# Second MoE: its second-layer products moved behind other first-layer products, their PSUM sums alternated per step, and the rounding copies of its sums queued later

## The chip, the core and the metric

The program runs on one core of a Trainium2 chip. The metric is the device time of one execution in microseconds (us); times of several executions are given as a median. TensorE (PE in the rows, its weight loads PEld), VectorE (DVE), ScalarE (ACT) and GpSimd (POOL) each work through a queue of their own in order; SyncE (SP) issues the DMAs used here.

## What is computed

The reference chains three blocks over 2304 tokens of width 512, all in float32:

```python
x = _attn_ref(q, k, v)                       # linear attention, reshaped to 2304 x 512
for e in range(4):                           # first MoE: 4 experts, 512 -> 1024 -> 512
    h = np.maximum(x @ w1[e], 0.0)
    out += p[:, e:e + 1] * (h @ w2[e])
h = x @ w_in                                 # second MoE: 512 -> 2048 -> 512
g = np.where(h > 0.0, h, np.exp(np.minimum(h, 0.0)) - 1.0)
return g @ w_out
```

Each float32 matrix product is made of three products of rounded parts: a high part times a high part, high times low and low times high. A rounded high part is an ACT copy, the low part a subtraction of it from the value, mostly on POOL.

## The kernel before

Attention and the first expert come first (to about 704 us of the trace). Then follow 30 steps, `for i, (s, b) in enumerate(STEPS)`: s counts ten quarters of 512 hidden units (s = 0 to 5 the other three experts, s = 6 to 9 the second MoE), b three blocks of 768 tokens. Steps 18 to 29 are the second MoE; the row that starts at 802.8 us is step 18, and step 29 starts at 1194.9 us.

**First layer of a step.** It is a seven-product scheme (Strassen-Winograd) over two halves `fp` of the hidden units: 14 products, called p0 to p13 here (`product`, 6 matmuls each, L1146). Four PSUM banks A to D hold a half; B collects four of the products, and VectorE and ScalarE copy or add banks between them: p0 is copied to `s5` (ACT L1424), p1's bank B to bank A (ACT L1427, "the first layer's copy"), D becomes B + s5 after the third product (DVE L1431), C becomes B + s5 after the fifth (DVE L1442). The halves swap the banks, so p7/p8 and the next step's p0/p1 write banks of the half before.

**Activation.** `elu` (L1184 to L1186, three ACT instructions) works on the four quarters A11, A22, A21, A12 of a half when their bank is done; its `rest` (DVE L1193, L1194) is queued with the next product by `run_pend`. In steps 21 to 29 (`fast(i)`, s = 7 to 9) the second layer is a seven-product scheme too, so `rest` also forms the sums S1, S2, S3 with A21 (DVE L1198 to L1200) and S4 with A12 (L1203). `parts` (ACT L1168, POOL L1169) makes the rounded high and low part of each quarter and sum; `flush` queues what waits.

**Second layer.** The second-layer products of step i-1 stand between the first-layer products of step i. For steps 22 to 29 they are `turned_product(i-1, k)`, k = 0 to 6, 12 matmuls each (L1272), one behind each of the products in `PLACES`; they collect in two PSUM pairs X and Y, and DVE L1281 adds a finished one to `accs`. In steps 19 to 21 they are eight `group`s (L1245 to L1247, 12 matmuls, evacuated by ACT L1248), and in step 18 six `chunk`s of the first MoE. The last step's seven products stand alone at the end.

**Side work.** `tick` runs the entries of a table of 24 hooks a step; `MIXED` and `PLAIN` say up to which hook each product runs. On it stand the second MoE's weights: `w1_steps` (loads of the next quarter's first-layer weights, sums on DVE L773/L774 and POOL L778/L779, parts on ACT L757 and DVE or POOL L768), `w2_fast` (second-layer weights: sums DVE L807, parts ACT L798 and POOL L799) and, up to step 19, `turn_steps` (PE L950, ACT L951 and L968, DVE L979).

## Time and profile before

| | us |
|---|---|
| median of 3 executions (1254.35 to 1256.67) | 1254.52 |
| the profiled execution's own time | 1253.47 |
| its span, first to last instruction | 1251.6 |
| mean granted TensorE clock | 0.981 |
| steps 22 to 29 in the trace | 953.4 to 1226.0 |
| last seven second-layer products and the end | 1226.0 to 1251.6 |

A row of the timeline gives start, duration, engine, line, operation and tiles; square brackets hold the idle time of the engine before it and what ended that. A matmul's duration there is modelled and overlaps the next one's; the distance between two starts is what a matmul costs in a stream. The tables of waits count only the idle time itself, not a lower clock behind it.

### The profile page before, as it was taken

The numbers are of one execution on the slowest core, as the hardware profiler recorded it, in microseconds if no ns is written. First come the engines' busy times: TensorE is split into PE (matmuls) and PEld (weight loads), VectorE is DVE, ScalarE is ACT, GpSimd is POOL, SyncE is SP. The second block draws the span as 40 slices with busy tenths as digits, with TensorE's granted clock in tenths as the row PEclk, the third lists the DMA queues.
The fourth block names the chain that finished last, engine by engine and source line by source line (L and its number), as shares of the span: only waits on it lengthen the run. The fifth ranks groups of instructions, "written<-read, shape, count | busy, mean of one in ns | idle before, by whom it ended". The sixth has DMA issues, their size and how long they took to land.

```text
span 1251.6 us, 21084 instructions
## 1 busy us (share of the span) xinstructions
PE 1184.6 (95%) x7516; PEld 1126.3 (90%) x7516; DVE 906.8 (72%) x1516; ACT 676.1 (54%) x1430; POOL 651.1 (52%) x611
## 2 busy tenths in 40 slices
PE   7799999999999999999999999978999988989897
PEld 6788889889999999999999998868999977988897
DVE  6877887565877887877877865655557788787774
ACT  6544543244455554454554534546777656665662
POOL 4522552046476476575584632536247557556652
PEclk9999999999999999999999999989999989999898
DMA  9345557837777767676766679978655554644152
GB/s 268 109 143 171 187 196 245 307 116 258 251 254 253 248 243 261 224 247 241 245 247 244 218 279 325 322 233 262 239 182 193 206 194 168 231 157 173 53 225 89
DMA packets 157400, 272.35 MB, mean 218 GB/s; under 512 B 12784, under 2 KB 83952, under 8 KB 157296
## 3 DMA queue, kind: packets, MB, share of 16 engines
q1 hardware_dynamic: 155568, 267.87, 62.5%
q10 hardware_dynamic: 1728, 3.15, 0.7%
q8 instruction: 59, 0.97, 0.3%
q14 instruction: 45, 0.37, 0.1%
HBM read 224.83 MB, written 46.14 MB: 216 GB/s over the span
## 4 chain that ended last, share of the span: by engine, by line
PE 73%; DVE 12%; ACT 7%; issue 3%; DMA 3%; POOL 2%; SPq 0%; DVEq 0%; ACTq 0%; POOLq 0%
PE o L1361 18%; PE h L1146 13%; PE m L1146 13%; PE o L1272 7%; PE h L1005 7%; PE o L1005 6%; ACT half L1185 1%; DVE gt L1199 1%; DVE accs L1281 1%; DVE extra L1193 1%; PE o L1245 1%; PE o L1247 1%; PE o L1246 1%; DVE half L1200 1%; DVE half L1194 1%
## 5 line engine op out<-in xcount | busy, mean ns | idle before, releaser
L1146 PE MATMUL m<-xh,w1s 128*128 128x384 f32 x840 | 250.0, 341 | 12.1 <-DVE half L1194 7.8
L1146 PE MATMUL h<-xh,w1s 128*128 128x384 f32 x840 | 244.6, 337 | 9.9 <-DVE half L1194 6.2
L1146 PEld LDWEIGHTS m<-xh,w1s 128*128 128x128 f32 x840 | 156.3, 190 | 20.6 <-DVE half L1194 10.6
L1146 PEld LDWEIGHTS h<-xh,w1s 128*128 128x128 f32 x840 | 155.4, 189 | 12.5 <-DVE half L1194 6.5
L1146 PE MATMUL m<-xl,w1s 128*128 128x384 f32 x420 | 141.8, 338 | 0.0
L1146 PE MATMUL h<-xl,w1s 128*128 128x384 f32 x420 | 141.1, 336 | 0.0
L1005 PE MATMUL o<-w2t,hpa 128*128 128x512 f32 x432 | 118.4, 401 | 0.8 <-DVE hpa L1037 0.5
L1005 PE MATMUL h<-xh,w1t 128*128 128x256 f32 (+1 forms) x512 | 112.0, 297 | 0.1
L1005 PEld LDWEIGHTS h<-xh,w1t 128*128 128x128 f32 x512 | 86.1, 192 | 5.2 <-POOL w1t L442 0.3
L1361 PE MATMUL o<-w2g,xh 128*128 128x256 f32 x540 | 90.4, 282 | 0.0
L799 POOL TENSOR_TENSOR w2g<-r,w2g 128x512 fp32r<-128x512 f32 x56 | 75.8, 1362 | 26.1 <-ACT w2g L798 26.1
L1005 PEld LDWEIGHTS o<-w2t,hpa 128*128 128x128 f32 x432 | 75.6, 189 | 14.9 <-DVE hpa L1037 2.4
L1361 PE MATMUL o<-w2g,hpa 128*128 128x256 f32 x540 | 89.0, 282 | 0.0
L1361 PE MATMUL o<-w2g,xl 128*128 128x256 f32 x540 | 87.3, 282 | 0.0
L1383 DVE SCALAR_TENSOR_TENSOR accs<-o,pn,accs 128x256 f32<-128x256 f32 x180 | 75.7, 474 | 14.8 <-PE o L1361 14.2
L1146 PEld LDWEIGHTS m<-xl,w1s 128*128 128x128 f32 x420 | 79.8, 190 | 0.4
L1146 PEld LDWEIGHTS h<-xl,w1s 128*128 128x128 f32 x420 | 79.5, 189 | 0.5
L1361 PEld LDWEIGHTS o<-w2g,xh 128*128 128x128 f32 x540 | 78.0, 190 | 0.1
L1005 PE MATMUL h<-xl,w1t 128*128 128x256 f32 (+1 forms) x256 | 77.3, 302 | 0.0
L1361 PEld LDWEIGHTS o<-w2g,hpa 128*128 128x128 f32 x540 | 76.1, 190 | 0.1
L1361 PEld LDWEIGHTS o<-w2g,xl 128*128 128x128 f32 x540 | 75.6, 190 | 0.2
L1272 PE MATMUL o<-hpa,w2g 128*128 128x384 f32 x216 | 53.5, 366 | 19.9 <-DVE accs L1281 19.9
(301 smaller groups left out, 3033.7 us busy)
## 6 DMA issues: line engine op xcount, KB each, us to landing
xh<-xs SPq DMA_DIRECT2D x210, 384.0 KB, 5.3
xl<-xs SPq DMA_DIRECT2D x210, 384.0 KB, 6.0
r<-in_w_dram SPq DMA_DIRECT2D x56, 256.0 KB, 4.7
xs<-stage SPq DMA_DIRECT2D x43, 256.0 KB, 3.1
xs<-xh SPq DMA_DIRECT2D x21, 384.0 KB, 4.1
xs<-xl SPq DMA_DIRECT2D x21, 384.0 KB, 4.1
r<-scratch SPq DMA_DIRECT2D x24, 256.0 KB, 4.1
x<-in_w_in_dram SPq DMA_DIRECT2D x10, 512.0 KB, 3.8
```

Source lines behind the costliest of these rows:

```text
L799: nc.gpsimd.tensor_tensor(out=t[:, 1], in0=src, in1=t[:, 0].bitcast(F32), op=ALU.subtract)
L1005: nc.tensor.matmul(out, lhsT, rhs, **kw)
L1146: nc.tensor.matmul(dst, t[:, wl, c + dl, :], x[xl_][:, dl, :], start=(n == 0 and p < 2), stop=(n == 5), skip_group_check=True,)
L1185: nc.scalar.activation(out=t, in_=m, func=AF.Tanh, scale=-0.5)
L1193: nc.vector.scalar_tensor_tensor(out=m, in0=m, scalar=1.0, in1=t, op0=ALU.add, op1=ALU.mult)
L1194: nc.vector.scalar_tensor_tensor(out=g, in0=h, scalar=0.0, in1=m, op0=ALU.max, op1=ALU.add)
L1199: tt(out=s2, in0=s1, in1=g11, op=ALU.subtract)
L1200: tt(out=g21, in0=g21, in1=g11, op=ALU.subtract)
L1245: nc.tensor.matmul(o, w[:, 0, :], gh, start=(f == 0), stop=False)
L1272: nc.tensor.matmul(y[:, m], l, r, start=(n == 0 and k in STARTS), stop=(n == 5), skip_group_check=True)
L1361: nc.tensor.matmul(o, l, r, start=(first_write and m == 0 and c != 1), stop=(m == 5), skip_group_check=True)
L1383: nc.vector.scalar_tensor_tensor(out=a, in0=sums[x][:, c * HALF_M : (c + 1) * HALF_M], scalar=pr, in1=a, op0=ALU.mult, op1=ALU.add)
```

## The change

The diff, cut to its core (`s4` is a tile of its own for S4, which before took S1's place; the stanza for steps 18 to 21 differs only in places and hooks):

```diff
-        ("A11", "B11", "Y", (0, 0)), ("S1", "T1", "X", (1, 1)), ("S2", "T2", "Y", (0, 1)), ("S4", "B22", "X", (0, 1)),
-        ("S3", "T3", "Y", (1, 1)), ("A12", "B21", "X", (0, 0)), ("A22", "T4", "Y", (1, 0)),
+        ("A11", "B11", (0, 0)), ("S1", "T1", (1, 1)), ("S2", "T2", (0, 1)), ("S4", "B22", (0, 1)),
+        ("S3", "T3", (1, 1)), ("A12", "B21", (0, 0)), ("A22", "T4", (1, 0)),
...
-    GROUP_PLACES = (2, 3, 4, 6, 8, 9, 11, 12)
+    GROUP_PLACES, TURNED_PLACES = (1, 2, 4, 6, 8, 9, 11, 13), (1, 2, 4, 6, 8, 11, 13)
...
         def sums2():
             f1, f2 = r[0][:, 0], r[0][:, 1]
-            nc.gpsimd.tensor_tensor(out=f2[:, 2:], in0=f2[:, 2:], in1=f1[:, :2], op=ALU.subtract)
-            nc.gpsimd.tensor_tensor(out=f1[:, 2:], in0=f1[:, 2:], in1=f2[:, 2:], op=ALU.subtract)
-
+            tt = (nc.vector if s > S_MOE else nc.gpsimd).tensor_tensor
+            tt(out=f2[:, 2:], in0=f2[:, 2:], in1=f1[:, :2], op=ALU.subtract)
+            tt(out=f1[:, 2:], in0=f1[:, 2:], in1=f2[:, 2:], op=ALU.subtract)
+
+        if s > S_MOE:
+            return {
+                -5: begin, -3: lambda: lo(0), -2: sums1, -1: lambda: hi(1), 1: lambda: lo(1), 2: sums2,
+                5: lambda: hi(2), 7: lambda: lo(2), 8: lambda: hi(3), 10: lambda: lo(3),
+            }
...
-            (8, w2_parts, "B11"), (14, w2_sum, "T1"), (16, w2_parts, "T1"), (18, w2_parts, "B22"), (19, w2_sum, "T3"),
-            (21, w2_parts, "B21"), (25, w2_sum, "T2"), (27, w2_parts, "T2"), (30, w2_parts, "T3"), (31, w2_sum, "T4"),
-            (34, w2_parts, "T4"),
+            (8, w2_parts, "B11"), (13, w2_sum, "T1"), (17, w2_parts, "T1"), (18, w2_parts, "B22"), (19, w2_sum, "T3"),
+            (21, w2_parts, "B21"), (24, w2_sum, "T2"), (28, w2_parts, "T2"), (30, w2_sum, "T4"), (31, w2_parts, "T3"),
+            (35, w2_parts, "T4"),
...
-                a1, b1 = (34, 39)
+                a1, b1 = (35, 40)
...
-        op, wname, x, (th, mh) = TURNED[k]
-        t, y = w2g[s, wname], sums[x][:, :, :TB]
+        op, wname, (th, mh) = TURNED[k]
+        t, y = w2g[s, wname], sums["XY"[(i + k) % 2]][:, :, :TB]
...
+    EARLY = {1: 4, 2: 8, 5: 12, 8: 16, 9: 20, 12: 24}
...
+    TURNED_HOOKS = {**MIXED, 0: 1, 10: 18, 11: 21, 12: 22}
...
-            fill = {n: (chunk, i - 1, c) for c, n in zip(CHUNKS, (1, 3, 5, 8, 10, 12))}
-        hooks = MIXED if fast(i - 1) or turned(i - 1) else PLAIN
+            fill = {n: (chunk, i - 1, c) for c, n in zip(CHUNKS, (1, 3, 5, 8, 10, 12) if moe else (1, 2, 5, 8, 9, 12))}
+        hooks = TURNED_HOOKS if turned(i - 1) else MIXED if fast(i - 1) else PLAIN if moe else EARLY
...
                         elu(i, B_, fp, "A12")
-                        flush()
+                        if not seven:
+                            flush()
```

Up to step 17 every engine's order is the same. From step 22 on, the second-layer products stand behind p1, p2, p4, p6, p8, p11, p13 (before p1, p2, p4, p6, p8, p10, p12), and since seven products alternate between two PSUM pairs and a step starts on the other one, the first product of a step no longer takes the pair of the last product of the step before. The parts of S1, S2, S3 are queued with those of S4 and A12, behind the copy of the first layer's next half.

On VectorE, from step 23's p12 or p13 into step 24's p1, stood before (`extra`, `half` and `gt` hold the activation's terms and quarters, `r` and `w1s` the next quarter's weights, m, h and o are PSUM banks):

```order
L768 TENSOR_TENSOR w1s<-r,w1s 128x512
L1193 SCALAR_TENSOR_TENSOR half<-half 128x384
L1194 SCALAR_TENSOR_TENSOR gt<-h,half 128x384
L768 TENSOR_TENSOR w1s<-r,w1s 128x512
L773 TENSOR_TENSOR r<-r 128x256
L774 TENSOR_TENSOR r<-r 128x256
L1193 SCALAR_TENSOR_TENSOR extra<-extra,half 128x384
L1194 SCALAR_TENSOR_TENSOR half<-m,extra 128x384
L1198 TENSOR_TENSOR gt<-half,gt 128x384
L1199 TENSOR_TENSOR gt<-gt 128x384
L1200 TENSOR_TENSOR half<-half,gt 128x384
L1281 TENSOR_TENSOR accs<-o,accs 128x768
```

and stands now (the first two `rest` rows are A22's, the next pair A21's, the last pair A12's; L1290 is the addition that was L1281, L1201 and L1202 were L1193 and L1194, L1212 was L1203):

```order
L768 TENSOR_TENSOR w1s<-r,w1s 128x512
L1201 SCALAR_TENSOR_TENSOR extra<-extra,half 128x384
L1202 SCALAR_TENSOR_TENSOR half<-m,extra 128x384
L1206 TENSOR_TENSOR gt<-half,gt 128x384
L1207 TENSOR_TENSOR gt<-gt 128x384
L1208 TENSOR_TENSOR half<-half,gt 128x384
L773 TENSOR_TENSOR r<-r 128x256
L774 TENSOR_TENSOR r<-r 128x256
L1201 SCALAR_TENSOR_TENSOR half<-half 128x384
L1202 SCALAR_TENSOR_TENSOR half<-h,half 128x384
L1212 TENSOR_TENSOR s_9736<-half,gt 128x384
L1290 TENSOR_TENSOR accs<-o,accs 128x768
```

The weight sums L773 and L774 moved behind A21's rows, and the addition of the step's last second-layer product moved behind A12's three rows; the rows of A22 and one L768 stand ahead of this piece.

On ScalarE, in the middle of step 24 (from the last `elu` instruction of A12 to the parts of the half), stood before (`hpa`, `xh`, `xl` hold the rounded parts):

```order
L1186 ACTIVATE half<-half 128x384
L1168 ACTIVATE hpa<-gt 128x384
L1168 ACTIVATE xh<-gt 128x384
L1168 ACTIVATE hpa<-half 128x384
L1424 ACTIVATE extra<-h 128x384
L1427 ACTIVATE m<-h 128x384
L1168 ACTIVATE xl<-gt 128x384
L1168 ACTIVATE xl<-half 128x384
```

and stands now (L1434 and L1437 were L1424 and L1427, L1174 was L1168):

```order
L1192 ACTIVATE half<-half 128x384
L1434 ACTIVATE extra<-h 128x384
L1437 ACTIVATE m<-h 128x384
L1174 ACTIVATE hpa<-gt 128x384
L1174 ACTIVATE xh<-gt 128x384
L1174 ACTIVATE hpa<-half 128x384
L1174 ACTIVATE xl<-s_9736 128x384
L1174 ACTIVATE xl<-half 128x384
```

The three copies of S1, S2 and S3 moved behind the first layer's copy; five copies of parts now follow it in a row.

## Rows read from the trace of the kernel before

**Rows 1.** The page's busy times: us, share of the span, instructions
```profile
PE 1184.6 (95%) x7516; PEld 1126.3 (90%) x7516; DVE 906.8 (72%) x1516; ACT 676.1 (54%) x1430; POOL 651.1 (52%) x611
```
**Rows 2.** Waits of TensorE from 860 us on: total us, times, longest us
```profile
PE o L1272 <- DVE accs L1281: 22.1, 10, 3.9
PE m L1146 <- DVE half L1194: 6.8, 8, 1.4
PE h L1146 <- ACT m L1427: 3.7, 3, 1.8
PE m L1146 <- ACT h L1427: 2.0, 2, 1.4
```
**Rows 3.** Stretches: length; busy PE, PEld, DVE, ACT, POOL; clock, DMA, GB/s
```profile
953.40:983.10 29.70, 29.55 (x170) 29.07 (x169) 24.74 (x35) 21.21 (x45) 21.28 (x18) 1.00 0.52 179
983.10:1015.80 32.70, 30.05 (x171) 29.09 (x170) 27.16 (x41) 21.48 (x46) 17.38 (x16) 1.00 0.56 200
1015.80:1053.00 37.20, 32.01 (x169) 30.96 (x168) 29.21 (x42) 22.98 (x49) 24.11 (x21) 0.91 0.49 174
1053.00:1089.20 36.20, 31.84 (x170) 31.19 (x170) 26.46 (x38) 23.04 (x49) 22.32 (x19) 0.91 0.46 158
...
1194.90:1226.00 31.10, 29.56 (x169) 28.82 (x167) 22.26 (x35) 20.00 (x43) 15.83 (x14) 1.00 0.49 189
1226.00:1251.60 25.60, 17.39 (x86) 16.85 (x84) 11.92 (x17) 4.55 (x10) 6.88 (x6) 0.87 0.20 77
```
**Rows 4.** TensorE's timeline: a product, a second-layer product, and four of its waits
```profile
978.97 0.33 PE L1146 MATMUL m<-xh,w1s 128*128 128x384 f32 x1
...
980.01 0.68 PE L1272 MATMUL o<-xh,w2g 128*128 128x384 f32 x3
...
982.09 0.33 PE L1146 MATMUL h<-xh,w1s 128*128 128x384 f32 x1
...
1018.15 0.44 PE L1146 MATMUL m<-xh,w1s 128*128 128x384 f32 x1 [1.19 <-DVE half L1194]
...
1022.52 1.33 PE L1272 MATMUL o<-hpa,w2g 128*128 128x384 f32 x3 [3.06 <-DVE accs L1281]
...
1230.11 1.33 PE L1272 MATMUL o<-hpa,w2g 128*128 128x384 f32 x3 [3.89 <-DVE accs L1281]
```
**Rows 5.** VectorE's timeline over the boundary of steps 23 and 24
```profile
1011.86 0.56 DVE L1442 TENSOR_TENSOR h<-h,extra 128x384 f32<-128x384 f32 x1
...
1017.53 0.56 DVE L1194 SCALAR_TENSOR_TENSOR half<-m,extra 128x384 f32<-128x384 f32 x1
...
1020.25 1.35 DVE L1200 TENSOR_TENSOR half<-half,gt 128x384 f32<-128x384 f32 x1
1021.52 0.95 DVE L1281 TENSOR_TENSOR accs<-o,accs 128x768 f32<-128x768 f32 x1
```
**Rows 6.** ScalarE's timeline in step 21, parts of sums ahead of the first layer's copy
```profile
938.84 0.53 ACT L1168 ACTIVATE xl<-gt 128x384 fp32r<-128x384 f32 x1 [1.04 <-DVE gt L1199]
```
**Rows 7.** Lines in steps 26 to 28 (1093.2 to 1198.9 us): ns min/median/max, first and last start
```profile
L1185 ACT ACTIVATE half<-extra x12: 525/526/528, 1100.3 to 1193.9; 128x384 f32<-128x384 f32 x12
...
L1194 DVE SCALAR_TENSOR_TENSOR half<-m,extra x3: 557/558/558, 1123.6 to 1195.7; 128x384 f32<-128x384 f32 x3
...
L1199 DVE TENSOR_TENSOR gt<-gt x6: 557/1040/1540, 1107.5 to 1197.0; 128x384 f32<-128x384 f32 x6
...
L773 DVE TENSOR_TENSOR r<-r x2: 426/834/1243, 1108.5 to 1122.2; 128x256 f32<-128x256 f32 x2
...
L1169 POOL TENSOR_TENSOR xl<-gt,xl x9: 1004/1314/1385, 1093.1 to 1198.8; 128x384 fp32r<-128x384 f32 x9
...
L799 POOL TENSOR_TENSOR w2g<-r,w2g x7: 1286/1297/1618, 1141.5 to 1186.5; 128x512 fp32r<-128x512 f32 x7
```
**Rows 8.** The same three steps as one stretch, columns as in rows 3
```profile
1093.20:1198.90 105.70, 93.45 (x504) 90.80 (x504) 82.86 (x120) 67.45 (x143) 63.88 (x56) 0.95 0.44 155
```
**Rows 9.** VectorE in step 18, the longest wait that the second MoE starts with
```profile
824.62 1.77 DVE L979 TENSOR_TENSOR stage<-accs,stage 128x512 fp32r<-128x512 f32 x1 [2.20 <-ACT stage L968]
```

More of the change, by code (lines that the diff above doesn't have):

```diff
@@ L1186, in elu @@
         nc.scalar.activation(out=m, in_=m, func=AF.Exp, scale=-1.0)
+        if fast(i) and "s4" not in halves:
+            halves["s4"] = tmp.tile([P, TB], F32, tag="ek", name="s4")
         g11, g22, s1, s2 = (gt[:, k] for k in range(4))
@@ L1202, in rest @@
             elif name == "A12":
-                tt(out=s1, in0=g12, in1=s2, op=ALU.subtract)
-                todo = [(("S4", fp), s1), (("A12", fp), g12)]
+                s4 = halves["s4"]
+                tt(out=s4, in0=g12, in1=s2, op=ALU.subtract)
+                todo = [(("S4", fp), s4), (("A12", fp), g12)]
             else:
@@ L1401, in tile_attention_moe_moe @@
     for i, (s, b) in enumerate(STEPS):
-        fill = {}
+        moe, fill = s < S_MOE, {}
         if fast(i - 1):
-            one = turned_product if turned(i - 1) else second_product
-            fill = {n: (one, i - 1, k) for k, n in enumerate(PLACES)}
+            one, places = (turned_product, TURNED_PLACES) if turned(i - 1) else (second_product, PLACES)
+            fill = {n: (one, i - 1, k) for k, n in enumerate(places)}
         elif turned(i - 1):
@@ L1416, in tile_attention_moe_moe @@
             f1, f2 = 2 * fp, 2 * fp + 1
-            moe = s < S_MOE
             for p in range(len(PRODUCTS)):
```

## The prediction

> **What bounds the kernel now.** I read the page's busy times first: TensorE stands at 95% [rows 1], so only its gaps can be won. Since the engines' orders differ from step 18 on, the waits of TensorE in that stretch come next [rows 2]: ten waits of second-layer products for VectorE's addition L1281 (22.1 us), eight of first-layer products for A21's activation L1194 (6.8), five for the first layer's copy L1427 (5.7). The table of stretches then gives each step [rows 3]. An undisturbed step is worked out from starts in the timeline: a first-layer product takes 1.04 us (978.97 to 980.01), a second-layer product 2.08 (980.01 to 982.09) [rows 4], so 14 and 7 of them make 29.1. Step 22 took 29.7, step 23 32.7, step 24 37.2, step 25 36.2, step 29 31.1 [rows 3]; steps 26 to 28 repeat 23 to 25. Steps 23 to 29 (983.1 to 1226.0, 242.9 us) are 39.1 over seven undisturbed ones. At 1226 the first-layer products end and the next start comes at 1230.11 [rows 4].
>
> A wait costs more than its idle time: steps 24 and 25 and the end show granted clocks of 0.91, 0.91 and 0.87 against 1.00 [rows 3], a stay at the lower of the two levels (1.2 against 2.4 GHz) behind idle times of 3 to 4 us. Behind the wait at 1230.11 three matmuls take 1.33 us where they take 0.68 at 980.01 [rows 4]; about twelve at twice the time cost some 2 us. The end therefore loses 3.9 + 2 = about 6 us, and steps 23 to 29 and the end together 45.
>
> **The change part by part.**
>
> *The alternating pair and the places.* Now the last product of a step collects in Y, its addition stands on VectorE behind A21's five rows, and the next step's first product, behind p1, wants Y again; that is the wait of 3.06 at 1022.52. With alternating pairs the first product finds its pair free, and the second one, behind p2, needs that addition: one second-layer product and one first-layer product later, 2.08 + 1.04 = 3.12 us. I replay the boundary of steps 23 and 24 with the new order, counting from p11's end: p1 of step 24 is due at 2.08 + 1.04 + 1.04 + 2.08 + 1.04 = 7.28, where it was due at 5.2, since a second-layer product moved from p10 to p11. VectorE's bank sum (0.56 [rows 5]) and ScalarE's three instructions on A22 at 0.53 each [rows 7] end at about 2.4, A11's copy at 2.9, two weight copies at about 0.6 each at 4.1, A21's three at 5.75. VectorE meanwhile has L768, A22's two, the addition of the sixth product (0.95 [rows 5]) and L768 again, until about 7.05, then A21's two at 0.56 [rows 7]: done at 8.25. p1 is 1.0 us late, against 1.35 now (1018.15: 1.19 idle). Then three sums at 0.56, two weight sums at 0.43 [rows 7], A12's three, and the addition: 13.6. The second product is due at 12.5 with p1's delay in it, so it waits 1.1. Sum for step 24: 2.2 us, against 8.1 now (37.2 less 29.1). That is with each instruction alone. L1199 shows 557 to 1540 ns and L773 426 to 1243 [rows 7], and in this chain L1200 took 1.35 [rows 5]; some five such prolongations in it give 6.3. I take the middle, 4.2, for steps 24 and 27.
>
> *Step 25 and 28.* The same replay without the next quarter's weights: A21 done at 6.4 (due 7.28), the addition at 10.8 (due 11.4), so the bank costs nothing, where 7.1 us go today. But T2's part, formerly on a hook ahead, is now queued on POOL behind the five subtractions S1, S2, S3, S4, A12, at 1.0 to 1.385 each [rows 7], and then takes 1.29 [rows 7]. From 9.5 this ends at 15.9 to 17.7; the third second-layer product wants it at 15.8: 0.1 to 1.9 us. With 1 us for the rest I bound it by 0.2 and 3, and take 1.5.
>
> *Steps 23, 26, 29.* Their 3.6, 3.5 and 2.0 us are a short L1194 wait, a pair wait of 1.3 and, in 23 and 26, one behind p10. All three have more than 2 us of new slack; 0 to 1.5 stays, since the weight copy on ScalarE ahead of the first layer's copy can still hold p9. I take 0.75. Step 22 has almost nothing to lose; I count -0.5 for T2's part there.
>
> *The end.* The addition of step 28's last product now follows A12's rows as well; with A21's five and A12's three rows at 0.58 it ends about 4.3 behind that product, and the second product is due at 2.08: 2.2 us, without a clock loss. The upper bound is 4.5; I take 3.2 of today's 6.
>
> *The copies of the sums.* S1, S2 and S3 are copied ahead of the first layer's copy today, and the copy of S2 alone waits 1.04 for VectorE [rows 6]; TensorE pays at p9 in steps 21, 24 and 27 (3.7 us [rows 2]). Behind the copy they cost nothing: S1's low part is wanted at the second product, 2.5 us behind A's copy, and needs 0.53 + 1.0 to 1.385. POOL, VectorE and ScalarE queue nothing behind them that TensorE wants sooner, but for T2's part above.
>
> *Sums of the weights on VectorE.* Four per three steps leave POOL and cost VectorE 0.43 to 1.24 each [rows 7], 1.7 to 5.0; they stand behind the addition, ahead of the third product's bank sum, which has 1.3 us to spare. POOL is not a bound. Weight loads move by one hook on SP; what is queued behind them, the next x tiles, is wanted half a step later. Nothing.
>
> *Steps 18 to 21.* A `group` between p1 and p2 covers the first layer's copy there (2.0 us in steps 20 and 21 [rows 2]), p9's wait of 1.8 in step 21 goes with the copies, and step 20's wait for L1194, about 1, gets two us of slack. Against that, step 21 has the weight work of step 24. Of these 5 us 0 to 5 are won; I take 3.5. Step 18's long wait hangs on ScalarE's and VectorE's chain through the stores of the first MoE (L979, 1.77 with 2.20 idle ahead of it [rows 9]), whose order there stays; the chunks and hooks move by one product. The wait at the head of step 19 moves from a transposition to p1. I count 0 for both, bounded by -4 and +4.
>
> *Sum.* What stays of the 45.3: 2 x 4.2 + 2 x 1.5 + 3 x 0.75 + 3.2 = 16.9, so 28.4 won; less 0.5, and 3.5 more: 31.4. The profiled execution's own 1253.5 becomes 1222; it stands 1 us below the median of 1254.5, which becomes 1223. With all lower bounds 38 + 5 + 4 = 47 are won (1207), with the upper ones 45.3 - 27.6 - 1.5 - 4 = 12 (1242).
>
> **The rivals.**
>
> *All covered.* The prolonged VectorE instructions are those that meet POOL's subtractions of S1 to S3; moved behind A21's sums, these meet additions out of PSUM instead (L1194, with one operand there, never left 557 to 558 [rows 7]). Then the lower bounds hold: about 1208. Against it: the replay leaves late points even with every instruction alone.
>
> *VectorE binds.* It is busy 82.9 of 105.7 us per three steps [rows 8]; with the sums 84.6, against TensorE's 87.4. Its idle 22.8 are waits for ScalarE and TensorE in a chain; if three quarters stay, three steps take 101.7, which wins 4.0 x 2.67 = 11, and with 5 at the end and in steps 20 and 21: about 1238. For it: A12, the addition and the next bank sum now stand in one row on VectorE.
>
> *VectorE and POOL hold each other up: slower.* By count VectorE has 21 additions at 0.95, 84 instructions at 0.557 and 14 on weights (8 us), 74.9 alone per three steps; the change makes it 76.6. Of these 66 read SBUF alone and are prolonged by about 0.82 (L773's 1243 less 426 [rows 7]) when they meet POOL. Today's 82.9 [rows 8] means about ten. POOL is busy 63.9 of 105.7, 60% [rows 8]; if they met it at that rate, 40 of 66, VectorE would need 109.4, and eight steps would be 10 us longer: 1264. It decides from 36 of 66 on. Against it: today's rate is a quarter of that, and POOL loses four sums.
> The Trainium skill ("SBUF — State Buffer", section "SBUF: two separate sides") states for this an exclusive lock: a VectorE instruction with two SBUF inputs and a GpSimd one cannot run together, and "the other fully blocks". That speaks against moving sums to VectorE, and by it alone the sum would be this rival's 1264. The trace agrees on which instructions grow (L1199, not L1194 [rows 7]).
>
> *The wait only moves.* If the addition came later by the 3.12 us that the pair wins, only the waits on the copy and on p10 would go, some 5 us: 1249. Against it: the two rows added ahead of it are A12's, 1.7 us, and L768 and A22 start earlier.
>
> **How the numbers follow.** Chances: forecast (1214 to 1232) 0.57; all covered 0.14; VectorE binds 0.17; the wait only moves 0.04; slower 0.06; no change 0.02. Predicted is the forecast's 1223. The range 1208 to 1241 leaves out what lies below all covered and the last three, about 0.17. Within 0.2% (2.5 us, about what a measurement of this kernel can tell from no change) lies 0.02; faster 0.92, slower 0.06.
>
> **What would show it.** In the profile after, the wait of L1272's successor for the addition should be under 8 us in all (22.1 now), none ahead of a step's first second-layer product; the wait of products for L1437 under 2; steps 25 and 28 at 30 to 31 us, 24 and 27 at 31 to 35; clocks of 1.00 in all of them; a new short wait for POOL's L805 in steps 25 and 28. L1207 and L1208 at 0.56 mostly would speak for all covered; VectorE above 90% busy, with waits of TensorE spread over bank sums, for VectorE binding. I am wrong if steps 24 and 25 keep 36 us, or if step 18 or 19 grows by more than 4.

## The result, and the profile after

The changed kernel takes 1232.2 us (median of 4, 1231.2 to 1233.0) where the kernel before takes 1254.4 beside it: a ratio of 0.9821 with a 95% interval of 0.9803 to 0.9839, or 22.3 us less. Forecast were 31.4 us less and 1223. The profiled execution of after took 1233.0 us, its span is 1231.3.

The page's busy times, as [rows 1] of before:

```profile
PE 1180.8 (96%) x7516; PEld 1124.0 (91%) x7516; DVE 912.8 (74%) x1528; ACT 676.1 (55%) x1430; POOL 639.1 (52%) x599
```

VectorE has twelve instructions more and GpSimd twelve fewer. Line numbers have moved: L1146 is L1152 now, the second-layer product L1272 is L1281, its addition L1281 is L1290, the activation's L1193 and L1194 are L1201 and L1202, the bank sums L1431 and L1442 are L1441 and L1452, the subtraction L1169 is L1175. The waits of TensorE from 860 us on, total, times and longest, beside [rows 2]:

```profile
PE h L1152 <- DVE m L1441: 6.1, 4, 2.6
PE m L1152 <- DVE half L1202: 5.5, 4, 2.6
PE o L1281 <- DVE accs L1290: 4.0, 4, 2.9
PE o L1281 <- POOL w2g L805: 2.2, 3, 1.1
```

The ten waits for the addition, 22.1 us, have become four, of which the one at the end has 2.9. The 5.7 us for the first layer's copy are gone altogether. Two rows are new: GpSimd's L805, which was foreseen, and on top of the table the bank sum L1441, which was not. The stretches by step (22 to 28), columns as in [rows 3]:

```profile
951.16:982.24 31.08, 29.94 (x170) 29.03 (x169) 26.46 (x38) 23.21 (x49) 21.99 (x19) 1.00 0.49 175
982.24:1014.21 31.97, 29.42 (x169) 29.10 (x169) 25.07 (x40) 21.05 (x46) 14.19 (x15) 1.00 0.61 215
1014.21:1048.52 34.31, 31.27 (x169) 30.63 (x169) 31.52 (x46) 23.92 (x51) 24.44 (x20) 0.95 0.48 170
1048.52:1079.83 31.31, 30.02 (x169) 29.06 (x169) 26.14 (x40) 22.56 (x48) 21.57 (x19) 1.00 0.54 193
1079.83:1113.34 33.51, 30.96 (x169) 30.64 (x169) 25.87 (x41) 21.87 (x47) 14.98 (x15) 0.95 0.58 205
1113.34:1146.41 33.07, 30.00 (x169) 29.02 (x169) 30.58 (x45) 23.09 (x50) 23.83 (x20) 1.00 0.50 177
1146.41:1177.72 31.31, 30.00 (x169) 29.04 (x169) 26.17 (x40) 22.57 (x48) 21.61 (x19) 1.00 0.31 104
```

Step 25 went from 36.2 to 31.3 us, step 24 from 37.2 to 34.3, but steps 23 and 26, which the forecast put at 29.9, still take 32.0 and 33.5. The timeline of VectorE, GpSimd and TensorE in step 23 shows why:

```profile
1001.10 2.56 POOL L1175 TENSOR_TENSOR hpa<-gt,hpa 128x384 fp32r<-128x384 f32 x2 [3.07 <-ACT hpa L1174]
...
1003.58 0.41 DVE L768 TENSOR_TENSOR w1s<-r,w1s 128x256 fp32r<-128x256 f32 x1
1003.63 1.21 POOL L1175 TENSOR_TENSOR xh<-half,xh 128x384 fp32r<-128x384 f32 x1
1004.02 1.10 DVE L779 TENSOR_TENSOR r<-r 128x256 f32<-128x256 f32 x1
1004.80 1.18 POOL L1175 TENSOR_TENSOR xl<-s,xl 128x384 fp32r<-128x384 f32 x1
1005.16 1.10 DVE L780 TENSOR_TENSOR r<-r 128x256 f32<-128x256 f32 x1
1005.94 1.17 POOL L1175 TENSOR_TENSOR xl<-half,xl 128x384 fp32r<-128x384 f32 x1
1006.19 0.55 DVE L1441 TENSOR_TENSOR m<-h,extra 128x384 f32<-128x384 f32 x1
...
1006.79 0.45 PE L1152 MATMUL h<-xh,w1s 128*128 128x384 f32 x1 [2.55 <-DVE m L1441]
```

The two weight sums that the change put on VectorE stand ahead of L1441 and run beside GpSimd's row of five subtractions for S1, S2, S3, S4 and A12, the last three of which meet them; the change had queued those of S1 to S3 into that row. Each sum takes 1.10 us. p11 writes the bank that L1441 reads, and waits 2.55. In step 26 the wait is the same 2.55, but the granted clock stands at 0.55 in the 2.6 us behind it, where it stays at 1.00 in step 23; this accounts for the 1.5 us between the two steps. The head of step 24 has the same kind of meeting:

```profile
1014.35 1.42 DVE L768 TENSOR_TENSOR w1s<-r,w1s 128x512 fp32r<-128x512 f32 x1
1015.18 1.71 POOL L768 TENSOR_TENSOR w1s<-r,w1s 128x512 fp32r<-128x512 f32 x1
1015.70 1.62 DVE L1201 SCALAR_TENSOR_TENSOR extra<-extra,half 128x384 f32<-128x384 f32 x1
1017.42 0.56 DVE L1202 SCALAR_TENSOR_TENSOR half<-m,extra 128x384 f32<-128x384 f32 x1
```

L1201 takes 1.62 us beside GpSimd's L768, L1202, which reads PSUM, 0.56; p1 waits 2.61 for it.

### The profile page after: what moved, and what is told of

It reads as the page before. It is cut to its first block, busy times and chain, and to the rows that moved or that the text cites. A ratio compares the mean times of both kernels' runs of the same rounds, so it can differ in the third digit from the quotient of the medians.

```text
span 1231.3 us, 21098 instructions
## 1 busy us (share of the span) xinstructions
PE 1180.8 (96%) x7516; PEld 1124.0 (91%) x7516; DVE 912.8 (74%) x1528; ACT 676.1 (55%) x1430; POOL 639.1 (52%) x599
## 4 chain that ended last, share of the span: by engine, by line
PE 75%; DVE 9%; DMA 5%; ACT 4%; POOL 3%; issue 3%; SPq 0%; DVEq 0%; POOLq 0%; ACTq 0%
PE o L1370 18%; PE h L1152 14%; PE m L1152 14%; PE h L1011 7%; PE o L1011 6%; PE o L1281 5%; PE o L1256 1%; PE o L1254 1%; PE o L1255 1%; DMA xh<-xs 1%; DMA xs<-stage 1%; PE o L1235 1%; PE o L1234 1%; PE o L1236 1%; POOL w2g L805 1%
## 5 line engine op out<-in xcount | busy, mean ns | idle before, releaser
L1152 PE MATMUL m<-xh,w1s 128*128 128x384 f32 x840 | 247.8, 339 | 11.5 <-DVE half L1202 9.6
L1152 PE MATMUL h<-xh,w1s 128*128 128x384 f32 x840 | 245.7, 338 | 13.1 <-DVE half L1202 6.8
L1152 PEld LDWEIGHTS m<-xh,w1s 128*128 128x128 f32 x840 | 154.9, 189 | 18.3 <-DVE half L1202 11.5
L1152 PEld LDWEIGHTS h<-xh,w1s 128*128 128x128 f32 x840 | 155.7, 189 | 16.5 <-DVE m L1441 7.8
L1152 PE MATMUL h<-xl,w1s 128*128 128x384 f32 x420 | 141.4, 337 | 0.0
L1152 PE MATMUL m<-xl,w1s 128*128 128x384 f32 x420 | 141.1, 336 | 0.3 <-DMA xl<-xs 0.3
L805 POOL TENSOR_TENSOR w2g<-r,w2g 128x512 fp32r<-128x512 f32 x56 | 79.5, 1425 | 15.9 <-ACT w2g L804 15.8
L1152 PEld LDWEIGHTS m<-xl,w1s 128*128 128x128 f32 x420 | 79.2, 189 | 1.1 <-DMA xl<-xs 0.6
L1152 PEld LDWEIGHTS h<-xl,w1s 128*128 128x128 f32 x420 | 79.7, 190 | 0.4
L1290 DVE TENSOR_TENSOR accs<-o,accs 128x768 f32<-128x768 f32 (+1 forms) x64 | 59.5, 936 | 11.7 <-PE o L1281 11.6
```

The lines of the kernel that those rows point to most:

```text
L805: nc.gpsimd.tensor_tensor(out=t[:, 1], in0=src, in1=t[:, 0].bitcast(F32), op=ALU.subtract)
L1152: nc.tensor.matmul(dst, t[:, wl, c + dl, :], x[xl_][:, dl, :], start=(n == 0 and p < 2), stop=(n == 5), skip_group_check=True,)
L1290: nc.vector.tensor_tensor(out=a, in0=y[:, ms], in1=a, op=ALU.add)
```

## The experiments

The theory taken into them: the alternation is the core of the gain, and the forecast lost its 9 us where weight sums and subtractions meet ahead of p11. The rivals: the places and the copies win by themselves; p11's wait is the price of the moved sixth product alone; VectorE has simply too much to do.

The stretch ahead of step 20 scatters by some 7 us from profile to profile (step 20 starts at 884.2 to 891.3 us, also where all of that stretch is alike; step 0 starts at 266 us in the trace of before, not at about 704), so the table gives, from each kernel's profiled execution, the span from step 20's start to the end beside the medians.

| kernel | median us (lowest to highest) | ratio to before, 95% | less than before, us | step 20 to end, us |
|---|---|---|---|---|
| before | 1253.9 to 1255.1, each beside its kernels | | | 366.6 |
| the change | 1232.2 (1231.2 to 1233.0) | 0.9821 [0.9803, 0.9839] | 22.3 | 342.9 |
| x1 alternation alone | 1234.3 (1232.4 to 1238.5) | 0.9839 [0.9820, 0.9859] | 20.8 | 344.6 |
| x13 alternation and copies | 1229.3 (1228.0 to 1231.1) | 0.9803 [0.9789, 0.9816] | 24.6 | 341.0 |
| x5 all but the alternation | 1254.3 (1251.9 to 1256.6) | 0.9994 [0.9981, 1.0007] | -0.3 | 365.1 |
| x4 all but the copies | 1244.7 (1241.8 to 1246.7) | 0.9918 [0.9900, 0.9936] | 10.4 | 355.9 |
| x3 all but the sixth product's move | 1239.2 (1236.6 to 1239.9) | 0.9870 [0.9852, 0.9889] | 15.9 | 349.0 |
| x2 all but the weight sums | 1226.8 (1224.0 to 1229.2) | 0.9774 [0.9754, 0.9794] | 28.3 | 337.5 |
| x6 weight sums behind L1441 | 1232.1 (1230.5 to 1235.1) | 0.9815 [0.9792, 0.9838] | 21.9 | 342.7 |
| x8 x2, L768 later, end early | 1229.8 (1225.5 to 1230.4) | 0.9792 [0.9770, 0.9813] | 24.2 | 339.5 |
| x10 x8, GpSimd's L768 later | 1224.9 (1221.0 to 1227.0) | 0.9752 [0.9727, 0.9776] | 29.1 | 336.5 |
| x11 x10, addition ahead of A12 | 1225.7 (1224.9 to 1226.5) | 0.9773 [0.9759, 0.9786] | 28.2 | 337.7 |
| x12 x11, T2's copies early | 1226.8 (1224.6 to 1230.3) | 0.9775 [0.9761, 0.9788] | 27.1 | 337.3 |
| x14 joined | 1223.4 (1221.9 to 1225.0) | 0.9751 [0.9736, 0.9765] | 31.0 | 335.2 |

**The alternation alone.**

```diff
-        t, y = w2g[s, wname], sums[x][:, :, :TB]
+        t, y = w2g[s, wname], sums["XY"[(i + k) % 2]][:, :, :TB]
```

> The kernel before with one change alone: the two banks of a second-layer product alternate from step to step, so that a step's first product never meets the bank of the last one. Places, copies, hooks and weight sums stay as before. Theory (alternation is the core of the gain, the rest prepares it): the ten waits for the addition, 22.1 us with about 11 us of slow clock behind them, shrink at the boundaries of the steps that start 24, 25, 27, 28 and at the end from 3 to 4 us each to about 1; 1234 to 1240 us, and the long waits of steps 20 and 21 stay. Rival (the wait only moves): the second product, one second-layer and one first-layer product later, meets the same late addition, and each wait shrinks by no more than part of 3.12 us; 1244 to 1250 us, with waits of 1 to 2 us at the second product.

The theory held, 1234.3. The waits of this kernel from step 20 on:

```profile
PE m L1146 <- ACT h L1427: 8.5, 6, 1.8
...
PE o L1272 <- DVE accs L1281: 4.3, 4, 1.8
PE h L1146 <- ACT m L1427: 3.7, 3, 1.8
```

The addition fell from 22.1 to 4.3 us. In its place 6.5 us more of waits for the first layer's copy came up (8.5 against 2.0), but short ones: the granted clock from step 20 on is 1.00, against 0.96 before.

**All but the alternation.**

```diff
-        t, y = w2g[s, wname], sums["XY"[(i + k) % 2]][:, :, :TB]
+        t, y = w2g[s, wname], sums["YX"[k % 2]][:, :, :TB]
```

> The changed kernel with the pair of banks fixed again (Y, X, Y, X, Y, X, Y in every step), all its places, copies and weight sums kept. Theory (the alternation carries the gain, and the new places even need it, since the addition now stands behind A12's rows too): a wait for the addition comes back at the first second-layer product of every step from 23 on and at the end, some 3 us each with 1 to 2 us of slow clock behind the longer ones, at eight places; 1255 to 1270 us, slower than the kernel before. Rival (places and copies win by themselves what is won): 1236 to 1245 us.

At the end the first product now overwrites the bank ahead of the addition of step 28's last, so that sum is left out, and this end lacks the wait that was expected there; the seven boundaries before it are as meant, with waits of 2.1 to 3.7 us. The table of waits has

```profile
PE o L1281 <- DVE accs L1290: 22.1, 8, 3.7
```

as many us as before the change, and the time is that of the kernel before. It fell just short of the expected 1255, but on the theory's side: without the alternation everything else is worth nothing (-0.3), with it the rest is worth 1.5 (22.3 less 20.8), which the intervals of the two do not tell from nothing.

**The weight sums back on GpSimd.**

```diff
-            tt = (nc.vector if s > S_MOE else nc.gpsimd).tensor_tensor
+            tt = nc.gpsimd.tensor_tensor
```

> The changed kernel with the four weight sums per three steps (L779, L780) back on GpSimd, everything else as changed. Theory (these sums, ahead of the bank sum L1441 on VectorE, make the new wait of 2.55 us at the eleventh first-layer product of steps 23 and 26): that wait falls under 0.7 us in both, with its slow clock of some 1.6 us, and steps 23 and 26 become 30 to 31 us long where they are 32.0 and 33.5; in all 1225 to 1229 us against 1232. Rival (the wait comes from the second-layer product that left the place ahead of it, whoever computes the weight sums): the wait stays at 2 us or more, 1231 to 1234 us. Second rival: GpSimd, which gets the sums back, is late with T2's low part or the third quarter's; new waits of products for it of 1 us and more, 1233 to 1238 us.

The theory held: 1226.8, steps 23 and 26 at 29.7 us, a little under what was expected. Step 23 here, to be laid beside the rows of after:

```profile
999.55 0.41 DVE L768 TENSOR_TENSOR w1s<-r,w1s 128x256 fp32r<-128x256 f32 x1
999.60 1.22 POOL L1175 TENSOR_TENSOR xh<-half,xh 128x384 fp32r<-128x384 f32 x1
999.88 0.55 DVE L1441 TENSOR_TENSOR m<-h,extra 128x384 f32<-128x384 f32 x1
...
1000.49 0.45 PE L1152 MATMUL h<-xh,w1s 128*128 128x384 f32 x1 [0.28 <-DVE m L1441]
```

L1441 follows L768 at once, p11 waits 0.28. GpSimd does the sums afterwards, in its own idle time. The second-layer product that left p10 is thus not enough for the wait.

**The sixth product back behind p10.**

```diff
-    ..., TURNED_PLACES = ..., (1, 2, 4, 6, 8, 11, 13)
+    ..., TURNED_PLACES = ..., (1, 2, 4, 6, 8, 10, 13)
```

> The changed kernel with one number changed: the sixth second-layer product stands behind the tenth first-layer product again and not behind the eleventh. Theory (the new wait at the eleventh product in steps 23 and 26 is the price of that move, since nothing stands between it and the tenth; its gain is 2.08 us more slack for the first products of the next step): the wait of 2.55 falls under 0.7 us, steps 23 and 26 shorten by 2 to 4 us each; the wait at the second product of steps 24 and 27 (2.6 and 1.8 us) grows by 1.5 to 2.1 us each with its clock loss, those two steps lengthen by 2 to 4 us each: 1229 to 1235 us in all, about no change. Rival (the move costs only): steps 24 and 27 do not lengthen; 1224 to 1228 us.

p11's wait fell to 0.52 as expected, so it needs both, the sums and the missing cover. But the time is 4 us above the expected range. The next step's products come 2.08 us sooner, and the additions they wait for do not:

```profile
PE o L1281 <- DVE accs L1290: 13.2, 8, 4.4
```

The second product of step 24 waits 3.9 us, those of steps 25 and 28 1.6, the one at the end 4.4. In the changed kernel the move of this one product is worth 6 to 7 us, where I had expected about no change.

**The copies ahead again.**

```diff
-                        if not seven:
+                        if not seven or i > 21 or fp == 0:
                             flush()
```

> The changed kernel with the rounding copies of S1, S2 and S3 ahead of the first layer's copy again, as before the change, in all halves from step 22 on and in the first halves of step 21. Theory (moving them keeps GpSimd's subtractions away from VectorE's sums and frees the copy from waiting for them): L1207, whose median is 557 ns in the changed kernel, goes back to about 1040 ns, waits of first-layer products for the copy L1437 of 1 to 2 us come back in steps 21, 24 and 27, and A21's chain ahead of the bank sums gets longer; 1237 to 1245 us. Rival (with alternating banks there is slack enough for either order): 1231 to 1234 us. Second rival (the copies are better ahead, since S1 is wanted by the second product): 1226 to 1230 us.

The time is the theory's, the mechanism half of it. L1207 is not what grows (mean 623 ns over steps 22 to 28, 766 in the changed kernel), and no wait for the copy came back. What grows is the row behind it, L768, L773 and L774, and half of the L1201 (28 of them take 26.4 us against 20.4). Here in step 23, with GpSimd's S1 and S2 now beside it:

```profile
996.64 2.72 POOL L1175 TENSOR_TENSOR hpa<-gt,hpa 128x384 fp32r<-128x384 f32 x2 [1.06 <-PE h L1152]
996.98 1.51 DVE L768 TENSOR_TENSOR w1s<-r,w1s 128x512 fp32r<-128x512 f32 x1
998.52 1.12 DVE L773 TENSOR_TENSOR r<-r 128x256 f32<-128x256 f32 x1
999.32 1.20 POOL L1175 TENSOR_TENSOR xh<-half,xh 128x384 fp32r<-128x384 f32 x1
999.68 1.12 DVE L774 TENSOR_TENSOR r<-r 128x256 f32<-128x256 f32 x1
...
1006.62 0.69 PE L1152 MATMUL h<-xh,w1s 128*128 128x384 f32 x1 [4.83 <-DVE m L1441]
```

and in the changed kernel, where GpSimd is idle until 1001.10:

```profile
999.42 0.68 DVE L768 TENSOR_TENSOR w1s<-r,w1s 128x512 fp32r<-128x512 f32 x1
1000.14 0.42 DVE L773 TENSOR_TENSOR r<-r 128x256 f32<-128x256 f32 x1
1000.60 0.42 DVE L774 TENSOR_TENSOR r<-r 128x256 f32<-128x256 f32 x1
```

Three instructions take 3.75 us instead of 1.52, all that stands behind them comes later, and p11 waits 4.83 instead of 2.55.

**Alternation and copies, in the old places.** The diff of x1, the copies' part of the change, and S4's own tile.

> The kernel before with two parts of the change: the alternating banks (1234.3 us alone) and the rounding copies of S1, S2 and S3 behind the first layer's copy, with a tile of its own for S4; all places, hooks and weight sums as before. Theory (what the places do is small; with alternating banks the copies are the rest of the gain, since in the kernel with alternation alone products wait 12.2 us for the first layer's copy): these waits fall under 4 us, 1224 to 1229 us. Rival (the copies need the new places, as the places need the copies): the copy cannot come sooner in the old places, since the product it waits for stands there, and S1's parts are late for the second product; 1232 to 1240 us.

1229.3 is just above the theory's upper edge of 1229, and better than the whole change by 2 to 3 us. The waits for the first layer's copy fell from 12.2 to 2.0 us. New are the products' waits for GpSimd, the low parts of S1 and of T2:

```profile
PE o L1275 <- POOL w2g L799: 3.0, 3, 1.1
PE o L1275 <- POOL xh L1169: 2.8, 1, 2.8
PE o L1275 <- POOL xl L1169: 2.8, 1, 2.8
```

The two of 2.8 us stand at the second product of steps 24 and 27, the S1 that the rival named; in the changed kernel, whose first products of a step are due 2.08 us later, neither stands. From step 22 on this kernel takes 274.7 us and x2, which adds the new places and hooks, 274.8: beside alternation and copies the new places win nothing there by these two profiles. The 3.5 us by which x2 is shorter from step 20 on lie in steps 20 and 21 (66.2 us here, 62.7 there).

**The weight sums behind L1441, still on VectorE.**

```diff
-                ... 1: lambda: lo(1), 2: sums2,
+                ... 1: lambda: lo(1), (2 if p else 4): sums2,
```

> The changed kernel, whose weight sums L779 and L780 stay on VectorE, with those of a next step's first quarter two hooks later, so that VectorE comes to them behind the bank sum L1441 and not ahead of it (steps 20, 23 and 26). Theory (their place in VectorE's queue is the harm, not their load): the wait at the eleventh product of steps 23 and 26 falls from 2.55 to under 0.7 us, these steps to 29.5 to 30.5 us, as with the sums on GpSimd; 1225 to 1229 us. Rival (VectorE's load is the harm): the two us come out at the bank sum behind or at the first products of steps 24 and 27, whose wait grows from 2.6 and 1.8 to 4 us; 1230 to 1234 us.

My theory fell, the rival held. p11's wait is 0.28, but L779 and L780 (0.87 and 1.12, again beside GpSimd) now hold up L1452 and the activations behind it, and the first products of steps 24 and 27 wait 3.9 us each instead of 2.6 and 1.8:

```profile
1008.33 1.12 DVE L780 TENSOR_TENSOR r<-r 128x256 f32<-128x256 f32 x1
1009.37 0.55 DVE L1452 TENSOR_TENSOR h<-h,extra 128x384 f32<-128x384 f32 x1
```

The 2 us are on the path in both places of VectorE's queue that were tried, ahead of L1441 and behind it.

**L768 later, and the addition at the end earlier,** from x2.

```diff
-                -5: begin, -3: lambda: lo(0), -2: sums1, ...
+                -5: begin, -3: lambda: None if p else lo(0), -2: lambda: (lo(0) if p else None, sums1()), ...
...
+    flush_adds()
     run_pend()
     flush()
     for k in range(len(TURNED)):
```

> The kernel with the weight sums on GpSimd (1226.8 us), and two orders on VectorE changed: the weight copy L768 that stands ahead of A21's rows at the heads of steps 24 and 27 now stands behind them, and at the end the addition of the seventh product of step 28 stands ahead of A12's rows. Theory (1.42 us of L768 in the queue is what makes the first products of steps 24 and 27 wait 2.48 us; A12's rows are what makes the second product at the end wait 2.9): the first wait falls to 0.5 to 1.2 us, steps 24 and 27 from 34.3 to 31.5 to 33 us, the last wait to 0.5 to 1.5; 1217 to 1223 us. Rival (L1201, itself 1.6 us because it meets GpSimd's L768, sets the wait): the wait at steps 24 and 27 stays at 2 us or more and only the end gains, 1223 to 1226 us.

Both waits fell as expected, at p1 from 2.48 to 0.80 and at the end from 2.90 to 0.35, and yet the time is neither the theory's nor the rival's; it is no shorter than x2's (1229.8 against 1226.8). The second products of steps 24 and 27 wait 3.8 us now. VectorE and GpSimd there:

```profile
1012.04 1.09 POOL L1175 TENSOR_TENSOR xh<-gt,xh 128x384 fp32r<-128x384 f32 x1 [1.87 <-ACT xh L1174]
1012.29 1.12 DVE L773 TENSOR_TENSOR r<-r 128x256 f32<-128x256 f32 x1
1013.09 1.19 POOL L1175 TENSOR_TENSOR xl<-gt,xl 128x384 fp32r<-128x384 f32 x1
1013.45 1.12 DVE L774 TENSOR_TENSOR r<-r 128x256 f32<-128x256 f32 x1
1014.25 1.17 POOL L1175 TENSOR_TENSOR hpa<-half,hpa 128x384 fp32r<-128x384 f32 x1
1014.49 1.34 DVE L1201 SCALAR_TENSOR_TENSOR half<-half 128x384 f32<-128x384 f32 x1
```

With p1's wait gone, the copies of S1 to S3 are released earlier, the moved L768 holds VectorE's row back, and so the subtractions meet the two sums and the first of A12's rows: 3.58 us for what takes 1.39 alone (0.42, 0.42, 0.55), all ahead of the addition.

**GpSimd's L768 later,** from x8.

```diff
-                ... 8: lambda: hi(3), 10: lambda: lo(3),
+                ... 8: lambda: hi(3), (10 if p else 13): lambda: lo(3),
```

> The kernel just named, with GpSimd's weight copy L768 of the next quarter behind its subtractions of S1 to S4 instead of beside VectorE's rows of A21. It prices the meeting of the two engines: VectorE's order is the same in both kernels. Theory (a VectorE instruction that reads SBUF alone is prolonged while GpSimd's runs): L1201 of A21 at the heads of steps 24 and 27 takes 0.55 to 0.6 us instead of 1.6, the wait of the first products falls by another 0.5 to 1 us, 1 to 3 us in all less than the kernel just named. Rival (L1201 is long for another reason): it stays at 1.4 to 1.6 us and the time is the same within 1 us. Against both: GpSimd's copy comes so late that the fifth product, which reads it, waits, 1 us or more.

From step 20 on it is 3 us shorter, the theory's size, but not at its place: L1201 still takes 1.29, beside another GpSimd instruction (L1175), p1 waits 0.81 as before, and it is the second product's wait that falls, from 3.8 to 2.9 in both steps. The one that changed is L1206, with L768 no longer beside it; VectorE's order is the same in both kernels. In x8:

```profile
1008.59 1.59 POOL L768 TENSOR_TENSOR w1s<-r,w1s 128x512 fp32r<-128x512 f32 x1
...
1009.66 0.92 DVE L1206 TENSOR_TENSOR gt<-half,gt 128x384 f32<-128x384 f32 x1
```

and in x10:

```profile
1014.30 0.56 DVE L1206 TENSOR_TENSOR gt<-half,gt 128x384 f32<-128x384 f32 x1
...
1016.55 0.42 DVE L773 TENSOR_TENSOR r<-r 128x256 f32<-128x256 f32 x1
1016.65 1.20 POOL L1175 TENSOR_TENSOR xh<-gt,xh 128x384 fp32r<-128x384 f32 x1 [3.39 <-ACT xh L1174]
```

This is the cleanest price of a meeting: 0.36 us on L1206, and 0.70 on L773, which now starts 0.10 us ahead of S1's subtraction and is not held.

**The addition ahead of A12's rows,** from x10.

```diff
                     nc.scalar.activation(out=s5, in_=C_, func=AF.Copy)
+                    flush_adds()
                     run_pend()
```

> The kernel of 1224.9 us (weight sums on GpSimd, L768 behind A21's rows, GpSimd's L768 late, end addition early) with the addition of every step's last second-layer product on VectorE ahead of A12's three rows at the next step's head, not behind them. Theory (the wait of the first product, once removed, became a wait of 2.9 us of the second product for that addition, because the moved L768 and the two sums behind it, up to 1.1 us each, stand ahead of A12's rows and these ahead of the addition): that wait falls to 0.3 to 1 us in steps 24 and 27, these steps from 35.6 to 31 to 33 us; from the start of step 20 to the span's end 329 to 333 us where the kernel just named takes 336.5; 1217 to 1222 us in all. Rival (the wait moves once more, now to the bank sum L1441 or to S4's copies, which come a us later): 335 us or more from step 20, 1223 us or more.

The rival held. The second product's wait fell to 0.30, but p11's rose to 1.3 to 1.8 (the addition at a step's middle is brought forward as well, ahead of the bank sum), and p4 waits 1.8 for GpSimd's L768, which comes too late once nothing else delays p4.

**T2's copies early,** from x11.

```diff
-            ... (24, w2_sum, "T2"), (28, w2_parts, "T2"), ...
+            ... (23, w2_sum, "T2"), (24, w2_parts, "T2"), ...
```

> The kernel just named with T2's sum one hook earlier and its rounding copies four hooks earlier, ahead of the subtractions of S1 to S4 in GpSimd's queue. Theory (the three waits of third second-layer products for T2's low part, 1.1 us in step 22 and 0.5 in steps 25 and 28, come from the queue of those subtractions): all three disappear, 2 to 3 us less from step 20 on than the kernel just named. Rival (ScalarE's copy of T2, 0.6 us, now stands ahead of the first layer's copy, and VectorE's sum, 0.8 us, ahead of A12's rows): the same time within 1 us, with new waits of first-layer products at the third or fourth place.

The three waits for T2's low part (3.1 us in x11) disappear as the theory says, the time does not: 337.3 us from step 20 on against 337.7, as the rival says, with its new waits of 0.5 us for the first layer's copy at p2 of steps 22 and 25.

**Joined.** x8 with T2's copies early and the addition ahead of A12's rows for `fp == 0` alone.

> The changed kernel with what the runs before it point to: weight sums on GpSimd; L768 behind A21's rows at the heads of steps 24 and 27; the addition of the last second-layer product ahead of A12's rows at a step's head and at the end, but not at its middle, where doing so cost 1.0 us at the eleventh product; T2's copies early; GpSimd's L768 in its place of the changed kernel, since its late place made the fifth product wait 1.8 us. Theory (each wait seen so far has a cause of its own in one queue, and with all of them gone no engine's load binds): waits of 0.8 us at the first product and 0.3 at the second in steps 24 and 27, 0.5 at the eleventh, none for GpSimd; from the start of step 20 to the span's end 328 to 333 us, where the kernel with T2's copies early takes 337.2 and the changed kernel 342.9; 1217 to 1222 us in all. Rival (VectorE's and GpSimd's chains are so tight that each gap closed opens another): 335 to 338 us from step 20, 1223 to 1228 us in all.

The lowest median of all, 31.0 us less than before and 8.7 more than the change (x10's interval overlaps its own), but by the rival's count: 335.2 us from step 20 on. p11 of steps 23 and 26 waits 0.28 again, so x11's wait there was the addition at the middle. In steps 24 and 27 new ones stand in the place of the old, 1.3 us at the second product, 1.0 at p8 and 1.8 at p11, and the top row of its waits is the bank sum once more:

```profile
PE h L1152 <- DVE m L1443: 4.2, 4, 1.8
```

## Why the forecast was right in sign and 9 us too large

Lengths in us; "forecast" is the length before less what the prediction takes off. (Its sum starts from 45.3 where its own parts, 39.1 and about 6, give 45.1; that changes nothing here.)

| steps | before | forecast | after | x2 |
|---|---|---|---|---|
| 18, 19 | 82.3 | 82.3 | 84.3 | 83.3 |
| 20, 21 | 68.4 | 64.9 | 62.7 | 62.7 |
| 22 | 29.7 | 30.2 | 31.1 | 30.8 |
| 23 | 32.6 | 29.9 | 32.0 | 29.7 |
| 24 | 37.3 | 33.3 | 34.3 | 34.3 |
| 25 | 36.2 | 30.6 | 31.3 | 31.4 |
| 26 | 32.6 | 29.9 | 33.5 | 29.7 |
| 27 | 36.8 | 33.3 | 33.1 | 34.3 |
| 28 | 36.3 | 30.6 | 31.3 | 31.3 |
| 29 and the end | 56.8 | 52.7 | 53.6 | 53.3 |

*The alternation* was judged rightly: no first product waits for the addition any more, and x1 and x5 give it 21 to 22 us, nearly the whole of the result. From step 20 on, laid end to end, the alternation takes off 22.0 us (x1), the copies 3.6 more (x13), the new places and hooks 3.5 (x2, all in steps 20 and 21), and the weight sums put 5.4 back.

*The weight sums* are the step that failed. The prediction read "the third product's bank sum, which has 1.3 us to spare" and counted nothing. That slack holds at p2, behind which a second-layer product stands. In the second half the change itself had taken the second-layer product from between p10 and p11, so that there the bank sum had no cover. The sums beside GpSimd's subtractions cost 1.10 us each, within the 0.43 to 1.24 that the prediction allowed them; two of them are 2.2 us, more than the 1.3 to spare, so that its own bounds did not support the nothing. Steps 23 and 26 came out 5.7 us above the forecast together, more than half of the 9.5 by which the table misses; x2, without the sums on VectorE, has both at 29.7. I had replayed the one boundary that waited before, not the row that the change lengthened.

*Steps 24 and 27* came out at 5.2 and 4.0 above an undisturbed step, where 4.2 was taken within 2.2 to 6.3. The size is right, the place is not: p1 takes 2.61 and 1.81 of it, where 1.0 was expected, and the second product next to nothing, where 1.1 was. Two rows that the replay took alone make p1's wait in step 24: L768 took 0.74 us and L1201 1.06 more than alone. The prediction also looked for clocks of 1.00 in all of these steps; steps 24 and 26 show 0.95. x8 shows that the two are one chain: with p1 free, the second product waits.

*Steps 25, 28 and 22*: 2.2 us stay in 25 and 28 where 1.5 was taken. Of these 1.3 are idle time, 0.53 the foreseen wait for T2's part, 0.5 at p1 and 0.24 for the addition; the rest stands mostly around these waits, each of which costs some 0.3 us more between starts than its idle time. Step 22 lost 1.4, not 0.5, with the wait for T2's part at 1.1.

*The end* waits 2.9 where 2.2 was the replay; x8 shows the cause named, A12's rows ahead of the addition. That it would come "without a clock loss" was wrong: the granted clock stood at 0.72 and 0.69 in the two products behind the wait, which take 2.9 us each instead of 2.1, so that the end lost some 4.6 us where 3.2 was taken and 4.5 was the bound.

*Steps 20 and 21* won 5.7, above the forecast's 3.5 and its upper 5; the four waits in them that were named are gone, 4.8 us of idle time. *Steps 18 and 19* lost 2.0 within the 4 allowed: in step 19 p1 waits 4.1 us for L1202, where before a transposition waited 3.2 and p1 1.0, and p8 has a new 0.9. What made those was not tried, and much of the 2.0 is scatter: x1 and x13, which leave these two steps as they were, have them at 83.0 and 84.2 us, x3 and x5, which leave them as changed, at 83.1 and 84.8.

*All covered* was tied to L1207 and L1208 at 0.56, and mostly they are (minimum and median of L1207 557 and 558 ns, though three of 14 took 1.53 us), but all was not covered: the meetings moved on to L779, L780, L768 and L1201. That sign was too narrow. *VectorE binds* named waits spread over bank sums, and the top row of waits is one. VectorE works 82.6 of the 97.9 us of steps 26 to 28, against 82.9 of 105.7 [rows 8], 84% and not above 90. In x2 it works 79.0 of 95.3; the waits are those of a chain in order, not of a full engine. The *slower* rival's rate did not come: 6 us of prolonging in these three steps (82.6 less 76.6) are about 7 meetings at the prediction's 0.82 us each, not 36.

## What to carry to other kernels

Before a bank is written again, count what stands between its last reader and that write in each place, and first where the change itself has taken cover away. Two changes can need each other: the alternation was worth 20.8 us alone, the rest nothing without it, and the copies 12 in the new places (x4) where they were 3.8 in the old (x13 against x1). A part's worth is thus measured beside the parts that it comes with. And an instruction on VectorE that reads SBUF alone should not come up while one of GpSimd's is under way, if TensorE waits behind it: it then moves at GpSimd's pace.

## What the runs showed of the hardware

A VectorE instruction with both operands in SBUF that starts while one of GpSimd's is under way ends a fixed time behind that one. With 256 columns this is 0.28 us (L779 and L780 in step 23 end at 1005.12 and 1006.26, the subtractions beside them at 1004.84 and 1005.98), with 384 columns 0.42 (L1201 in step 24, beside GpSimd's L768), with 512 columns 0.55. The fourteen profiles hold 573 such meetings from 951 us on with at least 0.3 us of GpSimd's instruction still to go, and all end within 0.01 us of these. One that starts first is not held: x2's L768 at 999.55 takes 0.41 us, though a subtraction starts at 999.60, and of 318 such cases in the same profiles none is prolonged. So what is left of GpSimd's instruction sets the price of a meeting, and a row of VectorE's moves on by one for each of GpSimd's: L779 and L780 start 1.14 us apart where L773 and L774 start 0.46 apart. GpSimd's own subtractions of 384 columns take 1.17 to 1.21 there and 1.01 alone (by the profile's page, spans on GpSimd are rough). Instructions with an operand in PSUM are untouched: from step 22 to the end of the changed kernel L1202 took 0.56 us in all of its 66 executions, 43 of them beside a GpSimd instruction, and L1290's additions of 768 columns 0.94 to 0.96. The Trainium skill ("SBUF — State Buffer", section "SBUF: two separate sides") calls this an exclusive lock, under which the other engine "fully blocks". The trace agrees, with the 573 meetings and the 318 above. The prediction weighed that rule as a reason for a general slowdown; it was right as a mechanism, and it cost where two rows met ahead of a wait.

The Trainium skill ("Perfetto Trace Analysis", section "Optimizing Scalar/DVE Operations") says that moving operations between these two engines "might not help". Here it did: the same twelve sums cost 5 to 6 us on VectorE, since they stood ahead of a bank sum, and nothing that shows on GpSimd, which had an idle place for them (TensorE's waits for GpSimd are 2.2 us in both kernels).
